# From group 2 on, six heads stay in place and two fill free rows: packing, weights, stores and PSUM banks of an outer-product attention with a maxout FFN

## The chip, the cores and the metric

The kernel runs on one core of a Trainium2 chip. The metric is the device time of one execution in microseconds (us), the median of three runs. Profiles are of one execution, taken by the hardware profiler. TensorE multiplies matrices, VectorE, ScalarE and GpSimd work element by element, and SyncE issues most DMA transfers.

## The reference

Four batches of eight heads, 768 steps, 48 features a head. Each head keeps a 48 x 48 state that a gate `f` decays by row; its output rows are put side by side to tokens of 384 features, which go through a maxout FFN with three input matrices.

```python
f = 1.0 / (1.0 + np.exp(-f_logit))
for t in range(S):
    state = f[:, :, t, :, None] * state + np.einsum('bhd,bhe->bhde', k[:, :, t], v[:, :, t])
    y[:, :, t] = np.einsum('bhd,bhde->bhe', q[:, :, t], state)
x = np.ascontiguousarray(y.transpose(0, 2, 1, 3)).reshape(B * S, H * D)   # 3072 x 384
h = np.maximum(np.maximum(x @ w1, x @ w2), x @ w3)                        # 3072 x 768
return (h @ w_out).astype(np.float32)
```

The weights come as 64-bit floats. They are loaded in 24 pieces of 384 KB and rounded to 32 bits on the chip.

## The kernel before

**Units and groups.** A unit is 64 steps of two batches (128 tokens); there are 24 units, and four make a group of 512 tokens, for which the FFN runs. In the code the groups count from 0, so "group 2 on" of the title is `g >= 1`.

**Attention, unit by unit.** `sigmoids` and `scan` build running products of the gate, `after` and `before` scale the keys and queries (kh, qh), `pairs` multiplies them, `values` applies the result to v, `sums` adds to the state. Two heads share the 128 partitions: one in rows 0 to 47, the other in rows 64 to 111; rows 48 to 63 and 112 to 127 hold zeros. From unit 8 on, the transposes run on VectorE (`turned`, L284, and `keys_by_blocks`, L370); before that they run on TensorE into two PSUM banks named `tr`.

**From attention to the FFN.** Group 0 makes x by tokens and transposes it (`y_by_tokens`, `x_of_tokens`). For the later groups `finish(u)` adds the state's part (L470) and copies the result with three ScalarE copies (L476) to `heads`: four pairs of heads, each in the padded layout. The FFN contracts over 384 features in three blocks of 128 rows, without padding. So `pack` moves `heads` to `xT` with ten transfers of 8 to 72 KB (L491): three units of a group at once when the third is done, then the last unit. The last pack of all goes half on SyncE's and half on ScalarE's queue.

**The FFN.** `ffn_first` runs group 0 with all three input matrices while the weights arrive; a buffer of 12 raw pieces (`raw`) holds what waits to be rounded. After its products, and between its four `outputs`, it prepares a cheaper form for the later groups: `apart` subtracts w1 from w2 and w3 on VectorE (L550), `turn` transposes w1 on TensorE and copies it back with ScalarE (L558), and `linear` forms w1 times w_out (L565, L569), kept as `w_lin` in the place of w1. The later groups (`ffn`) compute two products for each of six blocks of 128 hidden features: `product` (L511), three contraction blocks of 512 columns each, into a PSUM tile `p`; ScalarE takes the positive part of the first (L612) and VectorE the maximum with the second (L614). `p` has two banks. Then four `outputs`: the product of xT with `w_lin` (L528), the product of the hidden block with w_out (L532), a ScalarE copy (L537), and two stores of 64 tokens each (L542), one for each batch. A 32-bit matmul is two TensorE instructions in the profile.

**The order.** The program's order is written out by hand for every engine. A loop over the units places the attention's steps, and between them `fill(ns)` draws about as many nanoseconds of FFN work from a generator as it is told (2740 a step). SyncE's queue follows the program as well: for each unit it holds the loads of units ahead (L183 and L164), the pack, the stores, and reloads of weight pieces for a check of their range (`check_load`, L258, ScalarE at L267 to L270).

Of the kernel before, what the change touches and what calls it, by code (L numbers as in the profile page):

```python
# [9 lines left out]
FP32 = mybir.dt.float32  # L10
I32 = mybir.dt.int32
U32 = mybir.dt.uint32
# [34 lines left out]
C = 64  # L47
DP = 64
# [7 lines left out]
def kernel(  # L56
# [12 lines left out]
    nc = tc.nc  # L69
    B, H, S, D = q.shape  # L70
    HP = H // 2
    NU = B // 2 * (S // C)
    UT = 2 * C
    DM = H * D
    NK = DM // 128
    DFF = moe_w1.shape[1]
    NJ = DFF // 128
    GRP = 4
    TOK = GRP * UT
# [5 lines left out]
    w_in = [const.tile([128, NK, DFF], FP32, name=f"w_in{i}") for i in range(3)]  # L85
# [4 lines left out]
    def fast():  # L90
        ctx = ExitStack()
        with ctx:
            work = ctx.enter_context(tc.tile_pool(name="work", bufs=2))
            ps_tr = ctx.enter_context(tc.tile_pool(name="ps_tr", bufs=2, space=bass.MemoryType.PSUM))
# [63 lines left out]
            both = (nc.sync, nc.scalar)  # L158
# [34 lines left out]
            pieces = [(w_in[i][:, :, j * 128:(j + 1) * 128], src[:, j * 128:(j + 1) * 128])  # L193
                      for j in range(NJ) for i, src in enumerate((moe_w1, moe_w2, moe_w3))]
            pieces += [(w_out[:, j:j + 1, :], moe_w_out[j * 128:(j + 1) * 128, :]) for j in range(NJ)]
            RAW = 12
            PIECE = NK * 128
            raw, raw_next = {}, []

            def load_weights(count, done=0, queue=nc.sync):  # L200

                for n in range(len(raw_next), min(len(raw_next) + count, done + RAW, len(pieces))):
                    raw_next.append(n)
                    dst, src = pieces[n]
                    a = dst.shape[1]
                    if src.dtype != FP32:
                        raw[n] = work.tile([128, 2 * PIECE], U32, name="raw", bufs=RAW)
                        dst, src = raw[n].rearrange("p (a c) -> p a c", a=a), src.bitcast(U32)
                    queue.dma_start(out=dst, in_=src.rearrange("(a p) c -> p a c", a=a))

# [42 lines left out]
            def check_load(n):  # L253
                src = pieces[n][1]
                if src.dtype != FP32:
                    raw[n] = work.tile([128, 2 * PIECE], U32, name="raw", bufs=RAW)
                    a = pieces[n][0].shape[1]
                    nc.sync.dma_start(out=raw[n].rearrange("p (a c) -> p a c", a=a),  # L258
                                      in_=src.bitcast(U32).rearrange("(a p) c -> p a c", a=a))
# [171 lines left out]
                    else:  # L431
                        nc.vector.tensor_tensor(new, ds, d["state"].rearrange("p (a h) d -> p a (h d)", a=2), op=ALU.add)

            heads = keep.tile([128, HP, TOK], FP32, name="heads")

            def y_by_tokens(u):

# [21 lines left out]
                    nc.tensor.transpose(tr_x[:, kt, :], x[:, kt * 128:(kt + 1) * 128], ident)  # L459
                nc.scalar.copy(by_halves(xT)[:, u // 2, :, u % 2 * UT:(u % 2 + 1) * UT], tr_x)  # L460

            def finish(u):
                d = ready[u]
                y = d["y"]
                if u >= 2:
                    st = d["state"].rearrange("p (a h) d -> p a h d", a=2)
                    for hp in range(HP):
                        for par, a in FOUR:
                            r, o = slice(par * DP, par * DP + D), (par ^ a) * DP
                            nc.tensor.matmul(y[o:o + D, a, hp * C:(hp + 1) * C], lhsT=st[r, a, hp, :],  # L470
                                             rhs=d["qh"][r, a, hp, :], start=False, stop=(hp == HP - 1),
                                             skip_group_check=True)
                t0 = u % GRP * UT
                for par, a, n in ((0, 0, 2), (1, 1, 1), (0, 1, 1)):
                    i, o = slice(par * DP, (par + n) * DP), slice((par ^ a) * DP, ((par ^ a) + n) * DP)
                    nc.scalar.copy(heads[o, :, t0 + a * C:t0 + (a + 1) * C],  # L476
                                   y[i, a, 0:HP * C].rearrange("p (h t) -> p h t", h=HP))
                ready.pop(u)

            def by_halves(xT):  # L480

                return xT.rearrange("p k t -> p (k t)").rearrange("p (two k t) -> p two k t", two=2, k=NK)

            def pack(u0, u1, xT, queues=one):

                t, n = slice(u0 * UT, (u1 + 1) * UT), 0
                for h in range(H):
                    for lo, hi in ((h * D, min(h * D // 128 * 128 + 128, h * D + D)), (h * D // 128 * 128 + 128, h * D + D)):
                        if lo < hi:
                            p0 = h % 2 * DP + lo - h * D  # L490
                            queues[n % len(queues)].dma_start(out=xT[lo % 128:lo % 128 + hi - lo, lo // 128, t],  # L491
                                                    in_=heads[p0:p0 + hi - lo, h // 2, t])
                            n += 1


            HALF = TOK // 2
# [1 line left out]
            COLUMN = 4 / 2.4  # L498


            def product(g, xT, j, i, t):
                w = t.stop - t.start
                p = ps_f.tile([128, TOK], FP32, name="p")[:, 0:w]
                for kt in range(NK):
                    if g:
                        rhs = xT[:, kt, :]
                    elif w < TOK:
                        rhs = by_halves(xT)[:, t.start // HALF, kt, :]
                    else:
                        rhs = by_halves(xT)[:, :, kt, :]  # L510
                    nc.tensor.matmul(p if g or w < TOK else p.rearrange("p (two t) -> p two t", two=2),  # L511
                                     lhsT=w_in[i][:, kt, j * 128:(j + 1) * 128], rhs=rhs,
                                     start=(kt == 0), stop=(kt == NK - 1))
                    if kt == 1 and w == TOK:
                        yield 2 * w * COLUMN
                return p
# [5 lines left out]
                return work.tile([128, TOK], FP32, name="top")[:, 0:w]  # L522

            def outputs(g, hm, i, xT=None):
                p = ps_f.tile([128, TOK], FP32, name="p")
                if g:
                    for kt in range(NK):
                        nc.tensor.matmul(p[:, 0:DM], lhsT=xT[:, kt, i * UT:(i + 1) * UT], rhs=w_lin[:, kt, :],  # L528
                                         start=(kt == 0), stop=False)
                    yield NK * DM * COLUMN  # L530
                for j in range(NJ):
                    nc.tensor.matmul(p[:, 0:DM], lhsT=hm[:, j, i * UT:(i + 1) * UT], rhs=w_out[:, j, :],  # L532
                                     start=(g == 0 and j == 0), stop=(j == NJ - 1))
                    if j == NJ // 2 - 1:
                        yield NJ // 2 * DM * COLUMN
                o = work.tile([UT, DM], FP32, name="o", bufs=3)
                nc.scalar.copy(o, p[:, 0:DM])  # L537
                c, bp = divmod(g * GRP + i, 2)
                for a in range(2):
                    t0 = (2 * bp + a) * S + c * C  # L540
                    last = g * GRP + i == NU - 1 and a
                    (nc.scalar if last else nc.sync).dma_start(out=out[t0:t0 + C, :], in_=o[a * C:(a + 1) * C, :])  # L542
                yield NJ // 2 * DM * COLUMN

            def apart(j):
# [6 lines left out]
            def turn(j):  # L552

                p = ps_f.tile([128, TOK], FP32, name="p")
                piece = w_in[0][:, :, j * 128:(j + 1) * 128]
                for a in range(NK):
                    nc.tensor.transpose(p[:, a * 128:(a + 1) * 128], piece[:, a, :], ident)
                nc.scalar.copy(piece, p[:, 0:DM].rearrange("q (a c) -> q a c", a=NK))  # L558
                yield DM * COLUMN

            def linear(a):

                p = ps_f.tile([128, TOK], FP32, name="p")
                for j in range(NJ):
                    nc.tensor.matmul(p[:, 0:DM], lhsT=w_in[0][:, a, j * 128:(j + 1) * 128], rhs=w_out[:, j, :],  # L565
                                     start=(j == 0), stop=(j == NJ - 1))
                    if j % 2:
                        if j == NJ - 1:
                            nc.scalar.copy(w_lin[:, a, :], p[:, 0:DM])  # L569
                        yield 2 * DM * COLUMN  # L570

            def ffn_first(xT):
# [23 lines left out]
                for i in range(GRP):  # L596
# [3 lines left out]
                    for j in range(i * NJ // GRP, (i + 1) * NJ // GRP):  # L600
                        yield from turn(j)
                for a in range(NK):
                    yield from linear(a)

            def ffn(g, xT):
# [30 lines left out]
                                     start=True, stop=True)  # L636

            def new_xT():
                return work.tile([128, NK, TOK], FP32, name="xT")

            CHECKS = 2 * GRP + 3
            STEP = NK * HALF * COLUMN
# [5 lines left out]
            with tc.manual_schedule():  # L648
# [79 lines left out]
                for u in range(GRP, NU):  # L728
# [2 lines left out]
                    keys(u)  # L731
                    keys_by_blocks(u, 2)
                    if u > GRP:
                        finish(u - 1)
                        if u % GRP == 3:
                            pack(0, 2, xT)
                        elif u % GRP == 0:
                            pack(3, 3, xT)
# [37 lines left out]
                    fill(PART - 1000 if u < 2 * GRP else PART)  # L776
                    keys_by_blocks(n, 1)
                fill(PART)
                finish(NU - 1)
                pack(3, 3, xT, both)  # L780
                pending.append(ffn(NU // GRP - 1, xT))
                fill(20000)
# [261 lines left out]
```

## Time and profile before

| | |
|---|---|
| median of three runs | 457.38 us (457.23 to 457.5) |
| profiled execution | 457.98 us, span 456.2 us |
| granted TensorE clock | 1.0 |
| TensorE busy | 432.9 us |
| products of the later groups (L511, 512 columns) | 432 instructions, 195.3 us |
| outputs (L532 and L528) | 408 instructions, 141.7 us |
| ScalarE copies of `finish` (L476) | 60, 22.1 us |
| pack transfers | 100, median 1.8 to 2.2 us from issue to landing |
| stores | 48, 96 KB each, 2.2 us |
| HBM read, written | 37.75 MB, 4.72 MB |

How to read it: the span is the time from the first to the last instruction on the core; the profiled execution's own time is 1.8 us longer. A line such as "PE p L511" names the engine, what it writes and the line of the kernel. A wait is put down to what ended it. Matmul ends are modelled, so starts tell more than ends. "SPq" is SyncE issuing a transfer; PE is TensorE, PEld its weight loads, DVE VectorE, ACT ScalarE, POOL GpSimd.

### The profile page before, as it was taken

What the parts mean: (1) busy time and instruction counts of PE and PEld (TensorE: products, weight loads), DVE (VectorE), ACT (ScalarE), POOL (GpSimd) and SP (SyncE); (2) the same over time, 40 slices, a digit from 0 to 9 for tenths busy, and PEclk for the clock granted to TensorE, in tenths of its full rate; (3) what the DMA queues carried; (4) which work ended last, traced back from release to release, by engine and by line L of the source; (5) the groups of instructions that cost most, each with busy time, mean ns of one, the idle gap of its engine ahead of it and who ended that gap; (6) DMA issues with size and microseconds to landing.
All of it is one profiled execution on the core that took longest, in us unless ns stands there. A gap on an engine that the chain in (4) does not pass through costs nothing.

```text
span 456.2 us, 10209 instructions
## 1 busy us (share of the span) xinstructions
PE 432.9 (95%) x4062; PEld 244.1 (54%) x4062; DVE 253.4 (56%) x510; ACT 150.1 (33%) x350; POOL 103.9 (23%) x125
## 2 busy tenths in 40 slices
PE   4989999999999999999999999999989999999995
PEld 3777655556554456554456654455544455544553
DVE  6976757556858569357779557759456520011100
ACT  2434757403312214414414524504324331111000
POOL 2153654403033033032033023023032120000000
PEclk9999999999999999999999999999999999999999
DMA  8889997202547733647763557643746003100011
GB/s 169 213 245 299 259 205 89 36 19 71 94 66 88 133 93 72 147 78 146 92 164 77 147 104 131 98 142 72 165 78 124 2 0 88 45 9 0 4 35 37
DMA packets 177140, 47.13 MB, mean 103 GB/s; under 512 B 154816, under 2 KB 175552, under 8 KB 177088
## 3 DMA queue, kind: packets, MB, share of 16 engines
q1 hardware_dynamic: 173616, 45.64, 47.6%
q10 hardware_dynamic: 3472, 0.79, 0.8%
q8 instruction: 33, 0.54, 0.5%
q14 instruction: 19, 0.16, 0.1%
HBM read 37.75 MB, written 4.72 MB: 93 GB/s over the span
## 4 chain that ended last, share of the span: by engine, by line
PE 84%; DVE 5%; ACT 4%; DMA 4%; issue 2%; SPq 1%; POOL 0%; ACTq 0%; DVEq 0%
PE p L511 42%; PE p L532 18%; PE p L528 7%; PE y L470 3%; PE p L565 3%; PE y L399 2%; PE y L424 2%; PE a L380 2%; DVE r L317 2%; DMA raw<-in_moe_w_out_dram 2%; ACT heads L476 1%; PE tr L279 1%; DMA xT<-heads 1%; ACT sig L299 1%; PE y L395 1%
## 5 line engine op out<-in xcount | busy, mean ns | idle before, releaser
L511 PE MATMUL p<-xT,w_in 128*128 128x512 f32 (+1 forms) x504 | 212.8, 569 | 7.5 <-ACT top L612 2.8
L511 PEld LDWEIGHTS p<-xT,w_in 128*128 128x128 f32 x504 | 92.0, 190 | 104.2 <-issue 85.2
L532 PE MATMUL p<-w_out,hm 128*128 128x384 f32 x288 | 99.3, 491 | 1.3 <-ACT w_in L558 1.0
L532 PEld LDWEIGHTS p<-w_out,hm 128*128 128x128 f32 x288 | 53.6, 190 | 37.1 <-ACT w_in L558 1.3
L370 DVE STREAM_TRANSPOSE ks<-kh 32x128 f32<-32x128 f32 x224 | 67.7, 302 | 3.5
L614 DVE TENSOR_TENSOR hm<-p,top 128x512 f32<-128x512 f32 x30 | 20.4, 681 | 80.9 <-PE p L511 80.5
L327 POOL COPY ends<-r 128x8 f32<-128x8 f32 x24 | 6.7, 279 | 187.0 <-DVE r L317 187.0
L612 ACT ACTIVATE top<-p 128x512 f32<-128x512 f32 x30 | 17.8, 594 | 91.9 <-PE p L511 91.9
L383 DVE TENSOR_TENSOR at<-a,mask 128x512 f32<-128x512 f32 x24 | 16.6, 692 | 48.8 <-PE a L380 48.8
L528 PE MATMUL p<-w_in,xT 128*128 128x384 f32 x120 | 42.4, 489 | 0.0
L537 ACT COPY o<-p 128x384 f32<-128x384 f32 x24 | 11.4, 477 | 93.6 <-PE p L532 90.1
L476 ACT COPY heads<-y 64x256 f32<-64x256 f32 (+1 forms) x60 | 22.1, 369 | 54.9 <-PE y L470 45.5
L328 POOL TENSOR_TENSOR kh<-kt,r 128x512 f32<-128x512 f32 x16 | 31.4, 1960 | 35.4 <-DVE kt L284 33.2
L317 DVE TENSOR_TENSOR_SCAN r<-gate,from_one 128x520 f32<-128x520 f32 x24 | 29.8, 1241 | 6.6 <-ACT gate L296 3.4
L528 PEld LDWEIGHTS p<-w_in,xT 128*128 128x128 f32 x120 | 22.5, 190 | 16.0 <-issue 1.9
L335 DVE TENSOR_TENSOR_SCAN prod<-gate,from_inv 128x520 f32<-128x520 f32 x24 | 30.2, 1257 | 0.0
L247 POOL TENSOR_TENSOR w_in<-top_bits,rest_bits 128x384 uint32<-128x384 uint32 x18 | 20.8, 1161 | 26.6 <-DVE top_bits L241 12.1
L339 POOL TENSOR_TENSOR qh<-qt,prod 128x512 f32<-128x512 f32 x16 | 18.8, 1176 | 6.2 <-DVE qt L284 6.2
L345 POOL TENSOR_TENSOR state<-st,ends 128x384 f32<-128x384 f32 x22 | 18.9, 857 | 0.2
L399 PEld LDWEIGHTS y<-at,v_ld 64*64 64x64 f32 x640 | 11.2, 134 | 13.0 <-issue 6.1
L380 PE MATMUL a<-qh,kh 48*64 48x64 f32 x768 | 15.7, 219 | 1.0 <-DVE qh L339 0.8
L470 PEld LDWEIGHTS y<-qh,state 48*48 48x48 f32 x640 | 10.3, 119 | 11.7 <-issue 11.7
(101 smaller groups left out, 366.3 us busy)
## 6 DMA issues: line engine op xcount, KB each, us to landing
raw<-in_moe_w_dram SPq DMA_DIRECT2D x36, 384.0 KB, 5.5
v_ld<-in_v_dram SPq DMA_DIRECT2D x48, 96.0 KB, 3.1
raw<-in_moe_w_out_dram SPq DMA_DIRECT2D x12, 384.0 KB, 4.9
out_dram<-o SPq DMA_DIRECT2D x47, 96.0 KB, 2.2
xT<-heads SPq DMA_DIRECT2D x30, 72.0 KB, 2.2
f_ld<-in_f_logit_dram SPq DMA_DIRECT2D x32, 64.0 KB, 2.7
k_ld<-in_k_dram SPq DMA_DIRECT2D x32, 64.0 KB, 2.7
q_ld<-in_q_dram SPq DMA_DIRECT2D x32, 64.0 KB, 2.9
```

The costliest lines, as they stand in the source:

```text
L247: nc.gpsimd.tensor_tensor(dst, by(top), by(rest), op=ALU.add)
L317: nc.vector.tensor_tensor_scan(r[:, 0:LEN][:, ::-1], flat(gate)[:, ::-1], flat(from_one)[:, ::-1], 1.0, op0=ALU.mult, op1=ALU.max)
L328: (nc.vector if u < BY_ROWS else nc.gpsimd).tensor_tensor(kh.rearrange("p h a t -> p a h t"), kt, by_batch(r[:, 1:LEN + 1].rearrange("p (x ...
L335: nc.vector.tensor_tensor_scan(flat(prod), flat(gate_tiles[u % 2]), flat(from_inv[u % 2]), 1.0, op0=ALU.mult, op1=ALU.max)
L370: nc.vector.transpose(ks[n * 32:(n + 1) * 32, :, par, e0:e0 + 32], kh[p0:p0 + 32, :, a, t0:t0 + 32])
L380: nc.tensor.matmul(p[t, par, hp * C:(hp + 1) * C], lhsT=kh[r, hp, a, :], rhs=qh[r, a, hp, :], start=True, stop=True)
L470: nc.tensor.matmul(y[o:o + D, a, hp * C:(hp + 1) * C], lhsT=st[r, a, hp, :], rhs=d["qh"][r, a, hp, :], start=False, stop=(hp == HP - 1), s ...
L476: nc.scalar.copy(heads[o, :, t0 + a * C:t0 + (a + 1) * C], y[i, a, 0:HP * C].rearrange("p (h t) -> p h t", h=HP))
L511: nc.tensor.matmul(p if g or w < TOK else p.rearrange("p (two t) -> p two t", two=2), lhsT=w_in[i][:, kt, j * 128:(j + 1) * 128], rhs=rhs, ...
L528: nc.tensor.matmul(p[:, 0:DM], lhsT=xT[:, kt, i * UT:(i + 1) * UT], rhs=w_lin[:, kt, :], start=(kt == 0), stop=False)
L532: nc.tensor.matmul(p[:, 0:DM], lhsT=hm[:, j, i * UT:(i + 1) * UT], rhs=w_out[:, j, :], start=(g == 0 and j == 0), stop=(j == NJ - 1))
L614: nc.vector.tensor_tensor(hm[:, j, :], p, top, op=ALU.max)
```

## The change

From `g >= 1` on, x stays in the layout that `finish` writes. `xT` grows from three blocks to four and `finish` writes to it, so `heads` is gone. Pairs 0 to 2 (heads 0 to 5) stay where they are; the 48 rows of head 6 and of head 7 are folded into the free rows 48 to 63 and 112 to 127 of the three blocks, 16 rows times three blocks. That takes two transfers a pack.

The weights must follow the new order of features. w_lin gets it in `turn`, where two copies with a permuted pattern replace one. The two difference matrices are moved once, with 20 transfers between SBUF tiles (`place`, on SyncE's queue, ahead of the three `linear`), to two new tiles `placed`, which before that serve as six of the twelve raw buffers. A tile is stored with one transfer for both batches, the very last with two as before. For `g >= 1` the PSUM tile of a product or an output is taken in turn from `tr` and from `p`, two banks each.

```diff
-            RAW = 12
+            RAW, RAW_KEPT = 12, 2 * NK
+            placed = [keep.tile([128, NK, 2 * PIECE], U32, name=f"placed{i}") for i in range(2)]
+            def new_raw(n=0):
+                n = n % RAW - (RAW - RAW_KEPT)
+                if n >= 0:
+                    return placed[n // NK][:, n % NK]
+                return work.tile([128, 2 * PIECE], U32, name="raw", bufs=RAW - RAW_KEPT)
...
-            heads = keep.tile([128, HP, TOK], FP32, name="heads")
+            MAIN, SPARE = 2 * NK * D, DP - D
+            def by_features(n, x):
+                if n == 0:
+                    return x[:, 0:MAIN].rearrange("q (m par d) -> q m par d", m=NK, par=2)
+                return x[:, MAIN:].rearrange("q (par p m) -> q m par p", par=2, m=NK)
+            def place(i, n):
+                src, dst = w_in[i + 1], placed[i].bitcast(FP32)
+                if n < 2:
+                    r0 = MAIN % 128 + n * D
+                    nc.sync.dma_start(out=dst[n * DP + D:(n + 1) * DP], in_=src[r0:r0 + D, NK - 1, :])
+                    return
+                hp, par = divmod(n - 2, 2)
+                h = 2 * hp + par
+                for lo, hi in ((h * D, min(h * D // 128 * 128 + 128, h * D + D)), (h * D // 128 * 128 + 128, h * D + D)):
+                    if lo < hi:
+                        p0 = par * DP + lo - h * D
+                        nc.sync.dma_start(out=dst[p0:p0 + hi - lo, hp, :],
+                                          in_=src[lo % 128:lo % 128 + hi - lo, lo // 128, :])
...
-                    nc.scalar.copy(heads[o, :, t0 + a * C:t0 + (a + 1) * C],
+                    nc.scalar.copy(xT[o, :, t0 + a * C:t0 + (a + 1) * C],
...
-                for h in range(H):
-                    for lo, hi in ((h * D, min(h * D // 128 * 128 + 128, h * D + D)), (h * D // 128 * 128 + 128, h * D + D)):
-                        if lo < hi:
-                            p0 = h % 2 * DP + lo - h * D
-                            queues[n % len(queues)].dma_start(out=xT[lo % 128:lo % 128 + hi - lo, lo // 128, t],
-                                                    in_=heads[p0:p0 + hi - lo, h // 2, t])
-                            n += 1
+                for par in range(2):
+                    p0 = par * DP
+                    queues[par].dma_start(out=xT[p0 + D:p0 + DP, 0:NK, t], in_=xT[p0:p0 + D, NK, t])
...
+            def new_bank(g):
+                banks[0] += g > 0
+                if banks[0] % 2:
+                    return ps_tr.tile([128, TOK], FP32, name="tr")
+                return ps_f.tile([128, TOK], FP32, name="p")
+            def weight(g, i):
+                return placed[i - 1].bitcast(FP32) if g else w_in[i]
...
-                for a in range(2):
-                    t0 = (2 * bp + a) * S + c * C
-                    last = g * GRP + i == NU - 1 and a
-                    (nc.scalar if last else nc.sync).dma_start(out=out[t0:t0 + C, :], in_=o[a * C:(a + 1) * C, :])
+                dst = out.rearrange("(b s) d -> b s d", s=S)[2 * bp:2 * bp + 2, c * C:(c + 1) * C, :]
+                if g * GRP + i < NU - 1:
+                    nc.sync.dma_start(out=dst, in_=o)
+                else:
+                    for a, queue in enumerate(both):
+                        queue.dma_start(out=dst[a], in_=o[a * C:(a + 1) * C, :])
...
-                nc.scalar.copy(piece, p[:, 0:DM].rearrange("q (a c) -> q a c", a=NK))
+                for n in range(2):
+                    nc.scalar.copy(piece.rearrange("q a (par d) -> q a par d", par=2)[:, :, :, (0, D)[n]:(D, DP)[n]],
+                                   by_features(n, p[:, 0:DM]))
...
                 for a in range(NK):
+                    for n in range(3 * a, min(3 * a + 3, 2 * NK + 2)):
+                        for i in range(2):
+                            place(i, n)
                     yield from linear(a)
...
-                return work.tile([128, NK, TOK], FP32, name="xT")
+                return work.tile([128, HP, TOK], FP32, name="xT")
```

More of the change, by code (lines that the diff above doesn't have):

```diff
@@ L206, in load_weights @@
                     if src.dtype != FP32:
-                        raw[n] = work.tile([128, 2 * PIECE], U32, name="raw", bufs=RAW)
+                        raw[n] = new_raw(n)
                         dst, src = raw[n].rearrange("p (a c) -> p a c", a=a), src.bitcast(U32)
@@ L255, in check_load @@
                 if src.dtype != FP32:
-                    raw[n] = work.tile([128, 2 * PIECE], U32, name="raw", bufs=RAW)
+                    raw[n] = new_raw()
                     a = pieces[n][0].shape[1]
@@ L460, in x_of_tokens, with finish @@
                 nc.scalar.copy(by_halves(xT)[:, u // 2, :, u % 2 * UT:(u % 2 + 1) * UT], tr_x)
-            def finish(u):
+            def finish(u, xT):
                 d = ready[u]
@@ L480, in by_halves @@
             def by_halves(xT):
-                return xT.rearrange("p k t -> p (k t)").rearrange("p (two k t) -> p two k t", two=2, k=NK)
+                return xT[:, 0:NK].rearrange("p k t -> p (k t)").rearrange("p (two k t) -> p two k t", two=2, k=NK)
             def pack(u0, u1, xT, queues=one):
-                t, n = slice(u0 * UT, (u1 + 1) * UT), 0
-                for h in range(H):
-                    for lo, hi in ((h * D, min(h * D // 128 * 128 + 128, h * D + D)), (h * D // 128 * 128 + 128, h * D + D)):
-                        if lo < hi:
-                            p0 = h % 2 * DP + lo - h * D
-                            queues[n % len(queues)].dma_start(out=xT[lo % 128:lo % 128 + hi - lo, lo // 128, t],
-                                                    in_=heads[p0:p0 + hi - lo, h // 2, t])
-                            n += 1
+                t = slice(u0 * UT, (u1 + 1) * UT)
+                for par in range(2):
+                    p0 = par * DP
+                    queues[par].dma_start(out=xT[p0 + D:p0 + DP, 0:NK, t], in_=xT[p0:p0 + D, NK, t])
             HALF = TOK // 2
@@ L498, in fast @@
             COLUMN = 4 / 2.4
+            banks = [0]
+            def new_bank(g):
[5 more added lines that the diff above has]
+                return placed[i - 1].bitcast(FP32) if g else w_in[i]
             def product(g, xT, j, i, t):
                 w = t.stop - t.start
-                p = ps_f.tile([128, TOK], FP32, name="p")[:, 0:w]
+                p = new_bank(g)[:, 0:w]
                 for kt in range(NK):
@@ L511, in product @@
                     nc.tensor.matmul(p if g or w < TOK else p.rearrange("p (two t) -> p two t", two=2),
-                                     lhsT=w_in[i][:, kt, j * 128:(j + 1) * 128], rhs=rhs,
+                                     lhsT=weight(g, i)[:, kt, j * 128:(j + 1) * 128], rhs=rhs,
                                      start=(kt == 0), stop=(kt == NK - 1))
@@ L524, in outputs @@
             def outputs(g, hm, i, xT=None):
-                p = ps_f.tile([128, TOK], FP32, name="p")
+                p = new_bank(g)
                 if g:
@@ L733, in fast @@
                     if u > GRP:
-                        finish(u - 1)
+                        finish(u - 1, xT)
                         if u % GRP == 3:
@@ L778, in fast @@
                 fill(PART)
-                finish(NU - 1)
+                finish(NU - 1, xT)
                 pack(3, 3, xT, both)
```

## The prediction

> **What bounds the kernel now.** I read the page first: TensorE is busy nearly all the time and carries the chain.
>
> ```profile
> span 456.2 us, 10209 instructions
> ...
> PE 432.9 (95%) x4062; PEld 244.1 (54%) x4062; DVE 253.4 (56%) x510; ACT 150.1 (33%) x350; POOL 103.9 (23%) x125
> ...
> PE 84%; DVE 5%; ACT 4%; DMA 4%; issue 2%; SPq 1%; POOL 0%; ACTq 0%; DVEq 0%
> ```
>
> The change takes no matmul away, so only time in which TensorE stands still can be won. I asked for its waits from 132 us on, where `ffn(1)` starts:
>
> ```profile
> PE p L511 <- ACT top L612: 2.8, 4, 0.7
> PE p L511 <- DVE hm L614: 1.9, 3, 0.6
> PE p L511 <- DMA xT<-heads: 1.8, 1, 1.8
> ```
>
> The first two are the two PSUM banks of `p`: a product waits until ScalarE or VectorE has read the bank. The third is one wait for `pack`, at 334 us. The seven bank waits are larger than they look. In the chain's undisturbed piece
>
> ```profile
> 396.81 23.17 PE p L511 x54
> ```
>
> a 512-column matmul follows the last after 0.43 us, while its modelled end lies 0.60 us after its start (mean of the group), so each wait hides 0.17 us more: 4.7 + 7 x 0.17 = 5.9 us, and two starts that come 0.2 us late without a visible gap make 6.2. The `pack` wait is 2.0 in the same way. Together 8.2 us can be won.
>
> Then the SyncE queue and TensorE where group 0 ends (start, length, count):
>
> ```profile
> 105.62 6.30 SPq L491 DMA_DIRECT2D xT<-heads  x10
> ...
> 119.11 2.51 SPq L542 DMA_DIRECT2D out_dram<-o  x4
> 121.71 6.93 SPq L491 DMA_DIRECT2D xT<-heads  x10
> 128.74 1.44 SPq L164 DMA_DIRECT2D v_ld<-in_v_dram  x2
> 130.24 4.33 SPq L183 DMA_DIRECT2D k_ld<-in_k_dram  x8
> ```
> ```profile
> 127.89 4.14 PE L565 MATMUL p<-w_out,w_in 128*128 128x384 f32 x12
> 131.86 4.46 PE L511 MATMUL p<-xT,w_in 128*128 128x512 f32 x10
> ```
>
> An issue between two SBUF tiles costs the queue 0.63 us, and `ffn(1)` follows `linear` with no gap: whatever `ffn(1)` needs and `linear` only now orders has little time. Last, transfers by stretch (the last two columns are the busy share of the 16 transfer engines and GB/s):
>
> ```profile
> 296.90:301.20 4.30, 4.30 (x11) 1.91 (x11) 2.74 (x7) 0.60 (x1) 2.80 (x3) 1.00 1.09 318
> 440.00:443.00 3.00, 3.00 (x11) 1.74 (x10) 0.00 (x0) 0.20 (x1) 0.00 (x0) 1.00 0.30 66
> 453.43:453.93 0.50, 0.00 (x0) 0.00 (x0) 0.00 (x0) 0.00 (x0) 0.00 (x0) 1.00 0.70 232
> ```
>
> The middle one holds one output tile alone: 0.30 x 16 x 3 us = 14.4 us of engine time for 192 KB.
>
> **Four banks.** Products and outputs of groups 1 to 5 take turns over four banks, so a product may start while the three before it wait to be read, over 2 us of cover where the longest wait was 0.9. `tr` has no other user after unit 7 but the final check. Gain 6.2 us; late next are VectorE's key transposes (0.5 us in two waits). If the engines that read the banks are themselves late, half of it.
>
> **Packing.** Ten issues (6.3 us) become two (1.3 us). Only the wait at 334 us reaches TensorE, so the gain is at most 2.0 us; before the other groups' first products the old outputs fill 6 to 10 us, which hid the packs. The copies of `finish` go to `xT` in place of `heads`, the same three a unit. They write a buffer that the FFN two groups back has read: `ffn(1)`'s last product with it ends before 198.7 us, unit 12's copies come after 203.9, so no new wait.
>
> **Turn.** One ScalarE copy of 384 columns (478 ns) becomes two of 288 and 96. From 372 ns for 256 columns and 479 for 384, a column costs 0.84 ns and a copy 158 ns before that: 400 + 239 = 639, 0.16 us more. Six turns; TensorE waits for this copy in two or three places (1.0 us at 107 us is one): +0.4 us.
>
> **Reordered weights.** Twenty new issues on SyncE of 144 KB each, ordered ahead of `linear(0)` (6), `linear(1)` (8) and `linear(2)` (6). Behind them wait `pack(3,3)`, the v, k and q loads. In program order the queue is then: last store of group 0 (its tile is ready at 117.2), 6 places, 2 packs, 2 v loads, 8 places, 8 k loads, 6 places. TensorE needs heads 4 and 5, placed last, at the third contraction block of the first product. For that product the fourth of the last six decides. Its issue: 117.9 + 17 x 0.63 + 1.3 + 1.4 + 4.3 = 135.6. Landing: packs of 72 KB take 2.2 us, I take 2.5, and 0.7 for the long issues that every such stretch has (6.93 against 6.30): 138.8. TensorE is there at 131.9 + 0.4 + 4 x 0.43 = 134.0. A new stall of 4.8 us; `finish(8)` and `pairs(9)` stand behind that matmul on TensorE, so every engine waits with it. Bounds: 3 (no long issue, landing 2.0) to 11 (1.0 us a transfer, as two raw loads at 39 us took).
>
> **One store a tile.** SyncE issues 23 times less, which nobody waits for. But the pattern is new: two batches of 64 rows on the HBM side, so its outermost count is 2. Every transfer of the trace has rows or tokens outermost, 16 to 128 of them. Ends: spread like today's stores, 14.4 / 16 = 0.9 us (nothing lost); or dealt out along the outermost count, half a tile to one engine. Half a tile is 98 KB; at the rate of one busy engine in the first and third stretch (318 / 17.4 = 18.2 and 232 / 11.2 = 20.7 GB/s) that is 5.4 or 4.7 us, and 7.2 us by the second. What the rows show is work dealt out over many engines where the outermost count is large, so I take the second end, at 4.9 us.
>
> What it costs then: those two engines also carry their part of every later transfer, in order. In the trace the issues name eight completion semaphores in turn, and each waits for its own: a store that lands late holds the eighth issue after it. Stores 2 and 3 of group 0, issued at 114.2 (after the pack at 106.0, 8 f loads and 2 v loads) and 117.2, end on these engines at 115.1 + 4.9 = 120.0 and 124.9, landed near 126: the eighth behind, the second pack, goes out at 126 in place of 122.3. All places behind it move by 3.6: the stall at `ffn(1)` becomes 8.4. At 315.7, 318.2 and 324.0, by the same walk along the queue, three stores come ahead of the pack of group 4, plus two 384 KB check loads of 1.25 us an engine: 316.6 + 3 x 4.9 + 2.5 = 333.8, landed near 334.8, where TensorE asks at 332.5: the 2.0 us of `pack` are not won, +0.2. The last pack behind two stores: +0.9. Loads of k and q behind the stores come up to 7 us later, about their slack: 0 to 3, I take 0.
>
> [...]
>
> **Sum** for the forecast: -6.2 + 0.4 + 8.4 + 0.2 + 0.9 = +3.7 us. The profiled execution took 457.98 us, 1.8 more than its span; the median is 457.38, so I set the change on that: 461.0. By 4.7 us a store it is about +2.5; by 7.2 the terms are 13 for the stall, 7 and 5 for the packs, +19. As 7.2 comes from sixteen engines that read the same 64 rows at once, I give it little weight: its own range is 457 to 472.
>
> **Rivals.** (1) The store spreads over all engines. For it: today's stores of 64 rows do, at once. Then -6.2 - 2.0 + 0.4 + 4.8 = -3.0: 454.4 us, faster. It decides wherever a store takes less than about 4 us of one engine. (2) The store spreads, but placing is slow: 1.0 us each makes the stall 4.8 + 17 x 0.37 = 11, sum +3.3, 460.7; from 0.81 us a transfer on it eats the gain. For it: raw loads took 0.98 us in a full queue; against it, the stretch from 117 to 139 us has a busy share of only 0.49. (3) Four banks don't do what they say: the waits pass to the late engines, 3 us won in place of 6.2, store spread: 457.6, no change. Against it: ScalarE and VectorE idle 92 and 81 us waiting for TensorE's products.
>
> **How the numbers follow.** Chances: forecast 0.60, rivals 0.25, 0.08, 0.07. About 0.9 us (0.2%) is what can be told from no change. Faster: 0.23 of rival 1 and 0.05 from the forecast's low end, 0.28. Same: rival 3 and 0.03 of the rest, 0.10. Slower: 0.62. The range must reach rival 1 and into the forecast's upper bound: 454 to 470 leaves out a tenth at either end; the forecast alone, 457 to 472.
>
> **What would show it.** Bank waits (L511 behind L612 and L614) gone from 142 us on. A wait at the first product of `ffn(1)` of 8 us (forecast) or 5 (rival 1), ended by a place transfer. For the store, the stretch of a lone tile after 434 us: a share near 0.12 for 5 us and a landing of some 7 us says two engines; 0.7 for 1 us and 2.2 us to land says sixteen, and then I am wrong in sign.

## The result, and the profile after

The changed kernel takes 463.69 us (median of 6 runs, 462.23 to 465.2), the kernel before 457.44 in the same comparison: a ratio of 1.0132 (95% interval 1.0104 to 1.0159), which is 6.0 us slower. The profiled execution took 463.51 us.

The page of the changed kernel, the rows that answer to those of before:

```profile
span 461.8 us, 10115 instructions
...
PE 435.4 (94%) x4062; PEld 247.0 (53%) x4062; DVE 253.1 (55%) x510; ACT 150.4 (33%) x356; POOL 103.8 (22%) x125
...
PE 84%; DMA 4%; DVE 3%; issue 3%; ACT 2%; SPq 2%; POOL 0%; DVEq 0%; ACTq 0%
```

The matmuls are the same 4062. In the chain VectorE and ScalarE have given back 2% each, and the issues and SyncE have taken 1% each. Line numbers have moved: a product is L549 (L511 before), the outputs L566 and L570, the store L579, the pack L520, a place L457 or L464, the copies of `turn` L599. TensorE's waits from 130 to 470 us:

```profile
PE tr L549 <- DMA placed<-w_in: 7.9, 2, 6.3
PE tr L549 <- DMA xT<-xT: 2.8, 2, 2.1
PE y L433 <- DVE ks L379: 0.5, 2, 0.2
```

The waits for a bank are gone, as foreseen. The 1.8 us for one pack have become 2.8 for two, and `ffn(1)` waits for its placed weights. TensorE there (start, length, what was waited for), then SyncE's queue:

```profile
129.45 4.14 PE L607 MATMUL p<-w_out,w_in 128*128 128x384 f32 x12
133.57 1.10 PE L549 MATMUL tr<-xT,placed 128*128 128x512 f32 x2
136.35 1.12 PE L549 MATMUL tr<-xT,placed 128*128 128x512 f32 x2 [1.68 <-DMA placed<-w_in]
143.74 2.04 PE L549 MATMUL tr<-xT,placed 128*128 128x512 f32 x2 [6.26 <-DMA placed<-w_in]
145.57 2.72 PE L549 MATMUL p<-xT,placed 128*128 128x512 f32 x4
```
```profile
116.50 2.78 SPq L579 DMA_DIRECT2D out_dram<-o  x2
119.37 2.80 SPq L457 DMA_DIRECT2D placed<-w_in  x4
122.22 2.94 SPq L464 DMA_DIRECT2D placed<-w_in  x2
125.26 2.63 SPq L520 DMA_DIRECT2D xT<-xT  x2
...
129.84 5.07 SPq L464 DMA_DIRECT2D placed<-w_in  x8
134.96 4.38 SPq L183 DMA_DIRECT2D k_ld<-in_k_dram  x8
139.38 3.69 SPq L464 DMA_DIRECT2D placed<-w_in  x6
```

The third contraction block of the first product starts at 143.74. The forecast's walk along the queue ends there too: 138.8 and the store's 3.6 make 142.4, and this execution is 1.5 us late at the end of group 0. The store's hand in it is one row of SyncE's waits from 110 to 146 us, the second transfer of the pack:

```profile
SPq L520 <- DMA out_dram<-o: 0.8, 1, 0.8
```

What the forecast had not is in TensorE's next rows: the four matmuls from 145.57 on last 2.72 us, where four last 1.9 at full clock. Stretches of the trace (PE, PEld, DVE, ACT and POOL busy; then granted clock, busy share of the transfer engines, GB/s):

```profile
140.40:147.20 6.80, 3.46 (x4) 1.51 (x5) 0.00 (x0) 0.60 (x1) 0.00 (x0) 0.50 0.65 122
...
441.30:446.20 4.90, 4.90 (x17) 2.85 (x15) 0.00 (x0) 0.48 (x1) 0.00 (x0) 1.00 0.13 39
446.30:447.00 0.70, 0.70 (x4) 0.43 (x3) 0.00 (x0) 0.00 (x0) 0.00 (x0) 1.00 0.00 0
```

The clock is at half from 140.4, inside the standstill, until 147.2. And a lone output tile holds a share of 0.13 for 4.9 us and then nothing: two engines of sixteen (2/16 = 0.125). The trace does not name the engine of a packet, but this tile's 128 packets of 1536 bytes run two at once for 4.4 of its 4.9 us, and it closes with two writes to its semaphore, where each store of half a tile closes with sixteen. That is the test that the prediction named, and it came out for the forecast. What is ordered behind such a store lands late with it: the store ordered at 118.71 has its two writes after 8.5 us, and of the sixteen of the place ordered at 119.37 fourteen come after 2.7 to 4.1 us and two after 8.9 and 9.0.

Where the time goes stage by stage can be read from one mark in each group, the first ScalarE copy of its four outputs (for group 0 the last copy). In the profiled execution of before these marks stand at 116.7, 177.0, 243.6, 310.9, 377.8 and 433.9 us. The table has how much later (+) or earlier each kernel's profiled execution reaches them; the kernels below the first row are those of the experiments.

| kernel | end of group 0 | group 1 | 2 | 3 | 4 | 5 |
|---|---|---|---|---|---|---|
| changed | +1.50 | +10.08 | +8.23 | +6.06 | +4.82 | +5.71 |
| changed, again | -0.11 | +9.04 | +7.19 | +5.03 | +3.80 | +4.69 |
| two stores | +1.84 | +9.58 | +7.73 | +5.57 | +2.15 | +2.15 |
| two stores, TensorE busy | +1.59 | +7.34 | +5.49 | +3.33 | -0.08 | -0.08 |
| early places, one store | +1.47 | +2.12 | +0.27 | -1.89 | -1.04 | -0.15 |
| early places, two stores | -0.11 | -1.57 | -3.42 | -5.57 | -9.00 | -9.00 |
| early places, two stores, again | +1.70 | +0.21 | -1.65 | -3.80 | -7.22 | -7.22 |
| changed, TensorE busy | +1.59 | +9.77 | +7.92 | +5.76 | +4.54 | +5.43 |
| changed, store on ScalarE's queue | +0.46 | +8.90 | +7.04 | +13.02 | +19.57 | +20.58 |
| two banks | +1.57 | +11.48 | +11.47 | +11.45 | +13.24 | +14.14 |
| before, four banks | +1.44 | -0.45 | -2.31 | -4.45 | -6.12 | -6.11 |
| before, one store | +1.58 | +1.68 | +9.99 | +21.66 | +29.75 | +31.24 |

The 1.4 to 1.8 us in the first column are not an edit's: in these executions the clock is at half for 3.4 us near 31 us, in the others at full. The changed kernel and the one with early places and two stores have one profile of each kind. The kernel before has one profile, at full clock; its runs differ in their mean granted clock (0.993 to 1.0), so it seems to have both kinds. From the end of group 0 on, the change costs 8.58 in the stage of the placed weights, wins 1.85, 2.17 and 1.24, and loses 0.89: +4.2 (the repeat +4.8).

### The profile page after: what moved, and what is told of

Its sections match the earlier page's. It is cut to its first block, busy times and chain, and to the rows that moved or that the text cites. A ratio compares the mean times of both kernels' runs of the same rounds, so it can differ in the third digit from the quotient of the medians.

```text
span 461.8 us, 10115 instructions
## 1 busy us (share of the span) xinstructions
PE 435.4 (94%) x4062; PEld 247.0 (53%) x4062; DVE 253.1 (55%) x510; ACT 150.4 (33%) x356; POOL 103.8 (22%) x125
## 4 chain that ended last, share of the span: by engine, by line
PE 84%; DMA 4%; DVE 3%; issue 3%; ACT 2%; SPq 2%; POOL 0%; DVEq 0%; ACTq 0%
PE p L549 27%; PE tr L549 17%; PE p L570 10%; PE tr L570 8%; PE tr L566 4%; DMA xT<-xT 3%; PE p L566 3%; PE y L501 2%; PE y L408 2%; PE a L389 2%; PE y L433 2%; PE p L607 2%; SPq L464 1%; PE tr L288 1%; PE y L404 1%
## 5 line engine op out<-in xcount | busy, mean ns | idle before, releaser
L549 PE MATMUL tr<-xT,placed 128*128 128x512 f32 x180 | 85.6, 605 | 10.7 <-DMA placed<-w_in 7.9
L549 PE MATMUL p<-xT,placed 128*128 128x512 f32 x180 | 84.8, 602 | 0.0
L549 PEld LDWEIGHTS tr<-xT,placed 128*128 128x128 f32 x180 | 33.2, 191 | 50.1 <-issue 43.0
L570 PE MATMUL p<-w_out,hm 128*128 128x384 f32 x168 | 57.8, 491 | 1.3 <-ACT w_in L599 1.1
L549 PEld LDWEIGHTS p<-xT,placed 128*128 128x128 f32 x180 | 34.0, 192 | 40.8 <-issue 39.8
L549 PE MATMUL p<-xT,w_in 128*128 128x256 f32 (+1 forms) x144 | 51.4, 502 | 1.0 <-DVE hm L627 0.7
L570 PEld LDWEIGHTS p<-w_out,hm 128*128 128x128 f32 x168 | 31.2, 190 | 22.2 <-ACT w_in L599 1.3
L570 PE MATMUL tr<-w_out,hm 128*128 128x384 f32 x120 | 41.5, 490 | 0.0
L549 PEld LDWEIGHTS p<-xT,w_in 128*128 128x128 f32 x144 | 26.8, 196 | 16.6 <-issue 12.9
L570 PEld LDWEIGHTS tr<-w_out,hm 128*128 128x128 f32 x120 | 22.4, 190 | 14.9
L566 PE MATMUL p<-w_in,xT 128*128 128x384 f32 x60 | 21.3, 491 | 0.0
```

## Experiments

The theories were the forecast's (the store on two engines, whose late landing holds the places and the packs) and, as its rival, that placing by itself costs what was lost. A third came up with the clock. Each ratio is to the kernel before as measured beside that run (medians of 457.39 to 458.33 us), so differences between kernels are taken from the ratios.

**Two stores a tile** in the changed kernel:

```diff
-                if g * GRP + i < NU - 1:
-                    nc.sync.dma_start(out=dst, in_=o)
-                else:
-                    for a, queue in enumerate(both):
-                        queue.dma_start(out=dst[a], in_=o[a * C:(a + 1) * C, :])
+                for a, queue in enumerate(one if g * GRP + i < NU - 1 else both):
+                    queue.dma_start(out=dst[a], in_=o[a * C:(a + 1) * C, :])
```

> The changed kernel with two stores a tile again, 64 tokens each, all else as changed. Theory A (the one store runs on two transfer engines and holds up what is issued behind it): the lone tile at the end shows a busy share of 0.6 to 0.8 for 1 us in place of 0.12 for 5 us; the second pack of group 1 no longer waits some 2 us for its issue; the wait for the placed weights falls from 8.3 us to 3 to 5, the two waits for the packs (2.3 and 0.8 us) go. About 5 to 8 us less than the changed kernel, 454 to 458 us, so at or below the kernel before. Theory B (the placing alone is too slow, the store is innocent): the wait for the placed weights stays at 7 to 8 us, time 461 to 464.

Measured: 459.04 us, 1.0008 of before (0.9987 to 1.0029, 10 runs). The time lies between the two theories, 454 to 458 and 461 to 464. The waits for packs are gone; the one for placed weights is 6.4, over the 3 to 5 of theory A and under the 7 to 8 of B:

```profile
PE tr L549 <- DMA placed<-w_in: 6.4, 2, 6.2
```

So the store explains 1.0132 - 1.0008 = 0.0124, 5.7 us with an uncertainty of some 1.6, and the first rival's time of 454.4 was out of reach too. By the table the store costs 0.84 in the stage of the places, 2.18 at the pack of group 4 and 0.89 at the last: 3.9 between the two traces. The profiled execution with two stores was the longest of its ten, 0.8 over their median; the rest is within the uncertainty.

**The places earlier,** one store a tile as in the change: heads 6, 7, 0 and 1 ahead of `linear(0)`, the others ahead of `linear(1)`, first all of one matrix, then all of the other.

```diff
-                    for n in range(3 * a, min(3 * a + 3, 2 * NK + 2)):
-                        for i in range(2):
-                            place(i, n)
+                    if a == 0:
+                        for n in range(4):
+                            for i in range(2):
+                                place(i, n)
+                    elif a == 1:
+                        for i in range(2):
+                            for n in range(4, 2 * NK + 2):
+                                place(i, n)
```

> The changed kernel, with the twenty place transfers in another order: heads 6, 7, 0 and 1 ahead of the first linear step (8 transfers), heads 2 to 5 ahead of the second (12, those of the first product's matrix first), none behind the k loads. One store a tile stays. If what the first product waits for is only the place in SyncE's queue: its last transfer is issued about 6 us earlier (135 in place of 141), the wait falls from 8.3 us to 1 to 3 and the granted clock does not fall behind it, so 6 to 9 us less than the changed kernel, 455 to 458. If the placing is bound by the transfer engines and not by the queue's order: the wait stays above 5 us, 460 to 463.

Measured: 455.94 us, 0.9953 (0.9928 to 0.9978, 10 runs), 8.2 us less than the changed kernel by ratio. In the stage of group 1 the table has 0.65 in place of 8.58. The product waits 0.4 to 0.9 us in three places, and the clock stays full there. In the stage of group 4 the profiled execution loses 2.1 of it again: the pack's wait is 2.7 in place of 2.1, and the clock halves around its end. That execution is one of the longest of the ten (457.59); four are at 454.1 to 454.5, with a mean clock of 0.998 to 1.0.

**Both,** two stores a tile and early places:

> Both edits: two stores a tile, and the place transfers in the early order. By theory A nothing of the change's cost is left but two ScalarE copies a turn: bank waits (6.2 us) and the wait for the pack (2.0 us) gone, placing hidden, 449 to 451 us, 7 us faster than the kernel before. If a part of the cost sits elsewhere (the first 100 us, where the changed kernel was already 1.4 us late): 451 to 454.

Measured: 448.48 us, 0.9798 (0.9764 to 0.9832, 4 runs). TensorE's waits from 130 to 470 us are down to one row:

```profile
PE y L433 <- DVE ks L379: 0.5, 2, 0.2
```

It beats both kernels, and was run again for a narrower interval:

> The version with two stores a tile and the placing ahead of the first two linear steps, measured again for a narrower interval. It gave 0.9798 (0.9764 to 0.9832) of before. Expected: 448 to 450 us, 0.978 to 0.984.

Measured: 450.17 us, 0.9809 (0.9786 to 0.9833, 5 runs). That holds: 1.9% faster than before (1.7 to 2.1).

**Two banks** in the changed kernel, all else as changed:

```diff
-                if banks[0] % 2:
-                    return ps_tr.tile([128, TOK], FP32, name="tr")
```

> The changed kernel with its products and outputs on the two banks of p alone, all else as changed. If the four banks are worth what the waits before said: the nine late starts behind L612 and L614 come back, 6.2 us more than the changed kernel, 469 to 470 us. If the stall at the start of group 1 or the later waits for packs swallow part of them: 465 to 467.

Measured: 470.82 us, 1.0271 (1.0231 to 1.0311, 4 runs). The waits for banks are back, in six places where the kernel before has seven:

```profile
PE p L547 <- ACT top L655: 2.1, 3, 0.7
PE p L547 <- DVE hm L657: 1.9, 3, 0.6
```

By the table the stages of groups 2 and 3, where nothing else differs, cost 1.84 and 2.15 us more than in the changed kernel. In groups 1 and 4 half clock has a part: it lasted 10.2 us in place of 6.8 at the placed weights, and 3.4 more behind a pack.

**Four banks alone** in the kernel before:

```diff
-                p = ps_f.tile([128, TOK], FP32, name="p")[:, 0:w]
+                p = new_bank(g)[:, 0:w]
...
-                p = ps_f.tile([128, TOK], FP32, name="p")
+                p = new_bank(g)
```

> The kernel before with the four banks and nothing else of the change. By the prediction's step: the late starts behind L612 and L614 go, 6.2 us less than before, 451 to 452; the wait for the pack at 334 us stays at 2 us. If the waits pass on to engines that are late anyway: 3 us less, 454 to 455.

Measured: 451.83 us, 0.9880 (0.9863 to 0.9896, 4 runs), 5.6 us won. By the table 1.89, 1.86, 2.14 and 1.67 us in groups 1 to 4 are won, 7.6 from the end of group 0 on, of which some 0.5 is a pack wait that became shorter (1.3 in place of 1.8). The median has less. The profiled execution has the half clock near 31 us, and by the mean clocks (0.993 to 0.994 here, 0.997 to 1.0 beside) it fell on these four runs and hardly on those beside them.

**One store alone** in the kernel before, with its ten-transfer packs:

```diff
-                for a in range(2):
-                    t0 = (2 * bp + a) * S + c * C
-                    last = g * GRP + i == NU - 1 and a
-                    (nc.scalar if last else nc.sync).dma_start(out=out[t0:t0 + C, :], in_=o[a * C:(a + 1) * C, :])
+                dst = out.rearrange("(b s) d -> b s d", s=S)[2 * bp:2 * bp + 2, c * C:(c + 1) * C, :]
+                if g * GRP + i < NU - 1:
+                    nc.sync.dma_start(out=dst, in_=o)
+                else:
+                    for a, queue in enumerate(both):
+                        queue.dma_start(out=dst[a], in_=o[a * C:(a + 1) * C, :])
```

> The kernel before with one store a tile and nothing else of the change. Theory A (two engines, 4.9 us a store, later transfers queue behind it): a lone tile late in the run shows a busy share of 0.12 for 5 us; the wait for the pack at 334 us grows from 2 to 5 to 9 us and the packs of group 1 and of the last group come 0 to 3 us too late: 4 to 12 us more than before, 461 to 469. Theory B (spread over sixteen): 0 to 0.5 us less than before.

Measured: 488.07 us, 1.0664 (1.0646 to 1.0682, 4 runs): 30.7 us, far more than expected. TensorE's waits from 100 to 490 us, then SyncE's:

```profile
PE p L511 <- DMA xT<-heads: 12.1, 4, 7.5
PE p L511 <- DVE hm L616: 10.2, 5, 5.3
```
```profile
SPq L491 <- DMA out_dram<-o: 11.2, 5, 3.4
```

The second fence shows the mechanism: a transfer of a pack (L491) waits to be ordered until a store has landed, five times, up to 3.4 us. Ten transfers in a row pass the turn of all eight semaphores, so they meet every store that has not landed; two pass two of the eight. Late loads behind the packs have a part as well: VectorE, whose maximum ends the waits of the second row, itself waited from 190 to 330 us for loads of `f`:

```profile
DVE qt L284 <- DMA f_ld<-in_f_logit_dram: 15.5, 2, 9.3
```

Around the longer standstills (up to 7.5 us) the clock is at 0.50, for 27.2 us in four stretches. What this edit costs depends on what is queued with it: 31 us in one kernel, 4 to 6 in the other. That it is the two-transfer packs that shield the changed kernel from its own store fits these rows, but no run has those packs alone, so it is argued and not shown.

**The one store on ScalarE's queue** in the changed kernel:

```diff
-                    nc.sync.dma_start(out=dst, in_=o)
+                    nc.scalar.dma_start(out=dst, in_=o)
```

> The changed kernel, its one store a tile ordered on ScalarE's queue in place of SyncE's. The changed kernel stood at 1.0132 of before, with two stores a tile at 1.0008: 5.7 us for the store. Theory A: what costs is SyncE's queue, in which the eighth order after a store waits until the store has landed. Then the waits for the second copy into the free rows (2.3 and 0.8 us) go, the first placing wait (1.8) shrinks to 0.3, and the time is 459 to 460 us. Theory B: what costs is the two engines' own 4.9 us, in which they also carry a part of every later transfer, whatever queue ordered the store. Then the landings stay as late and the time stays at 462 to 464 us. A third outcome: ScalarE's own work waits behind the orders (0.6 us each, 23 of them) and it is slower than 464.

Measured: 478.58 us, 1.0426 (1.0395 to 1.0458, 4 runs), so A and B both missed, and the third outcome has the sign but not the cause: ScalarE was not what waited. SyncE's waits from 320 to 340 us, and ScalarE's queue:

```profile
SPq L183 <- DMA out_dram<-o: 12.2, 1, 12.2
```
```profile
331.20 0.52 ACTq L579 DMA_DIRECT2D out_dram<-o  x1
...
337.00 0.52 ACTq L579 DMA_DIRECT2D out_dram<-o  x1
```

A load of `f` on SyncE stood from 325.4 to 337.6 us for the store that ScalarE ordered at 331.20. Both name the same completion semaphore: the eight are handed out in one round over both queues (in the last pack of before SyncE's five transfers name the semaphores 100, 103, 105, 107 and 100, ScalarE's five between them 102, 104, 106, 108 and 102). On SyncE the store had at least been ordered ahead of the load; here the load also waits until ScalarE comes to order it, and the pack behind it went out at 344.3 and 345.0. The two pack waits grew from 2.8 to 12.0 us, and the half clock from 6.8 us to 23.9. It says once more that it is the turn of the semaphores that couples a late store to a later transfer; how much the two engines' own time adds is not told apart.

**TensorE kept busy** while it waits, first in the changed kernel (4 and 14 idle-filling multiplications ahead of the second and third contraction block):

```diff
+                    if g == 1 and j == 0 and i == 1 and kt:
+                        busy((0, 4, 14)[kt])
```

> The changed kernel with 4 and 14 matmuls of 256 columns that nobody reads put on TensorE where it waits for the placed weights (about 1.7 and 6 us of work, no more than the waits). If the granted clock falls because TensorE stands still for 6 us: it stays at 1.0 behind the stall, the five starts that came 0.43 us late behind it are on time, 1.5 to 3 us less than the changed kernel. If the clock falls for another reason: it still shows 0.5 there, and the time is that of the changed kernel or up to 1 us more.

Measured: 463.28 us, 1.0128 (1.0092 to 1.0164, 4 runs). The clock stayed at 1.0, and the four matmuls behind the stall took 1.88 us in place of 2.72. But the third block began 1.4 us later than without (145.17 against 143.74), and little was left: 0.4 us in the stage of group 1 (8.18 against 8.58). The transfer it waits for was ordered 1.5 us later in this execution (142.68 against 141.21): the second pack transfer waited 1.4 us for the store in place of 0.8, and one load of k took 1.41 us to order in place of 0.49. So the 1.5 to 3 us that were expected did not come.

Then with two stores a tile, where the late store does not disturb, 14 multiplications ahead of the third block:

> The changed kernel with two stores a tile, and 14 idle-filling matmuls on TensorE ahead of the third contraction block of the product that waits for the last placed weights, so that TensorE doesn't stand still there. Theory: the standstill of 6.4 us is followed by half clock, which makes five or six starts 0.42 us late each; with TensorE busy the clock stays at 1.0 and the time falls by 2 to 3 us from the 459.0 of two stores alone, to 456 to 457. Rival: the time of the starts is not lost on the path (the placed weights end later by as much, or something else is late next) and it stays within 0.5 us of 459.0.

Measured: 456.18 us, 0.9960 (0.9943 to 0.9977, 9 runs), 2.2 us less than two stores alone. TensorE there without, and with:

```profile
142.24 2.04 PE L549 MATMUL tr<-xT,placed 128*128 128x512 f32 x2 [6.20 <-DMA placed<-w_in]
144.08 3.62 PE L549 MATMUL p<-xT,placed 128*128 128x512 f32 x4
147.63 0.76 PE L501 MATMUL y<-qh,state 48*48 48x64 f32 x32
```
```profile
135.63 6.21 PE L679 MATMUL p<-from_one,ident 128*128 128x256 f32 x28
142.74 1.10 PE L551 MATMUL tr<-xT,placed 128*128 128x512 f32 x2 [0.90 <-DMA placed<-w_in]
143.68 1.88 PE L551 MATMUL p<-xT,placed 128*128 128x512 f32 x4
145.49 0.66 PE L501 MATMUL y<-qh,state 48*48 48x64 f32 x32
```

Both leave the standstill at nearly the same time (142.24 and 142.74), and by the attention's matmuls the busy one is 2.14 us ahead. So this part of the loss, 2.2 us with an uncertainty of some 1.2 by the ratios, is shown to be the clock's.

**The changed kernel again:**

> The changed kernel itself, so that it stands on the same chip as the others: 1.2 to 1.5% over the kernel before, with the stall at the start of group 1 of 8 us and a half clock behind it.

Measured: 462.98 us, 1.0123 (1.0102 to 1.0144, 4 runs). The places wait 1.9 and 6.2 us, the packs 2.2 and 0.7 (1.7, 6.3, 2.1 and 0.7 in the first profile); the half clock lasted from 136.6 to 146.9, longer than there.

## Why the prediction was right, step by step

The sign and the mechanism held; 463.7 lies inside the range and 2.7 above the figure.

- **Four banks, -6.2:** right, somewhat small. Taking them away from the change costs 0.0139 (6.4 us, half clock included), adding them to before gives 5.6 between medians and about 7 in the trace. The late engines took nothing over, so the third rival falls.
- **Turn, +0.4:** too large, about 0.1. The one wait of an output for this copy grew from 1.01 to 1.07 us, and the step from the last turn's matmuls to `linear` from 0.39 to 0.45.
- **Reordered weights, 4.8 of stall:** right in place, small in size. With two stores 6.7 us are lost there (gaps of 0.16 and 6.20, and twice the 0.17 that a gap hides). The fourth of the last six is ordered at 139.73 in that profile, which lags by 1.84 at the end of group 0: 137.9 against the 135.6 of the walk. Its landing, 2.4 us later, is near the 2.5 of the estimate. (It moves 96 KB; of the twenty, twelve move 144 KB, four 96 and four 48, where the prediction has 144 for all.) The mis-sized term is the queue, 2.3 us late where 0.7 had been set aside for long issues: an issue close behind the four places into 16 rows took 1.88 us where the others take 0.6, and the second store of the last tile, which the walk along one store a tile lacks, took another 0.6. Those four places took 3.5 to 5.8 us each to land where I took 2.5, and the two into 48 rows behind them 5.9; that the long issue comes from this is likely and not shown. This is the stretch with two stores:

```profile
124.00:128.00 4.00, 4.00 (x14) 2.30 (x13) 3.81 (x9) 0.48 (x1) 0.19 (x2) 1.00 0.99 127
```

All sixteen engines are busy (0.99) and yet move 127 GB/s; before, a share of 1.09 moved 318. The second rival had pointed that way (slow placing, argued down by a share of 0.49), but its price was per issue, and all issues but one stayed near 0.6 us. Why these transfers are slow was not told apart by a run.

- **The store's part of that stall, +3.6:** too large, 1.6 (8.3 lost, by gaps of 1.68 and 6.26, against 6.7). The second pack did go out late, at 127.3, less 1.5 of lag 125.8, where 126 had been worked out. The places behind it caught up with some of that. The stall as a whole, 8.3 against 8.4, is met by luck: two errors of opposite sign cancel.
- **Half clock, not in the sum:** some 2 us behind the standstill. The prediction priced a stall at its length alone. This is the term that was missing.
- **One store, two engines, 4.9 us:** as measured. That a store with an outermost count of 2 takes two engines was an estimate from rows with counts of 16 to 128; the lone tile's share of 0.13 for 4.9 us showed it. Packs: +0.2 net and +0.9 predicted; 0.3 (2.13 of gap and the hidden 0.17, against 2.0) and 0.9 measured. Nothing shows a cost of late loads of k and q, taken at 0.
- **First rival (454.4):** wrong in its condition. With the condition met, by two stores, the time is 459.0: it lacked the 1.9 us of stall and the clock as well.

Between the sum (+3.7) and the trace (+4.2 from the end of group 0 on) the errors mostly cancel: +2 for the clock and +0.1 for the packs, against 0.3 for the turn, 0.1 for the stall and about 1 us that four banks won beyond their term. In the profiled executions the early half clock adds 1.5, as this one had it and that of before had not; what is left up to the 6.0 of the ratio is within the spread of the runs.

## What to carry to other kernels

Before two stores are merged into one, look at the outermost count of the merged pattern: a count of 2 put 192 KB on two engines for 4.9 us, and the late landing was paid by transfers that have nothing to do with the store, 31 us in the kernel where ten-transfer packs follow it, 4 to 6 where two-transfer packs do. Order one-time moves well ahead of their first use: an earlier position in the same queue gave 8 us. Price a standstill of TensorE with the half clock that may come with it: in these traces the clock was at 0.50 in and behind the standstills of 6.2 to 6.5 us at the placed weights and around a pack wait of 2.7 us, and behind one of 6.2 us that cost another 2 us.

## What the hardware showed that was not expected

- The granted clock was 0.50 for 6.8 us (141.1 to 147.9 with two stores) in and behind a standstill of TensorE of 6.2 us (136.0 to 142.2). It was also 0.50 for 3.4 us around the end of a pack wait of 2.7 us, with early places and one store, and from 0.9 us behind the end of one of 2.2 us, with two banks. It stayed at 1.00 behind waits of 2.1 us in the changed kernel and 2.16 with TensorE kept busy. The first row is of early places, the second of two banks:

```profile
332.10:335.50 3.40, 3.12 (x4) 1.51 (x5) 0.84 (x3) 0.00 (x0) 0.24 (x1) 0.50 0.45 91
346.20:349.60 3.40, 3.40 (x6) 1.33 (x5) 0.11 (x1) 0.00 (x0) 0.00 (x0) 0.50 0.41 79
```

The stretches at half clock lasted 3.4, 6.8 and 10.2 us in these traces; what sets their lengths, and how long a standstill it takes, was not shown.

- Transfers of 144 KB into 16 rows in three blocks took 3.5, 4.0, 5.6 and 5.8 us to land one behind another (with two stores), the two into 48 rows close behind them 5.9 each, later ones into 48 rows 2.6 to 3.4 us.
- The eight completion semaphores are handed out in one round over both queues, so a store on ScalarE's queue held up a load on SyncE's for 12.2 us.
